# Chunk groups of five across batches, a fifth PSUM bank in the last block, and a new plan for a convolution with two expert layers

## The chip, the cores and the metric

The kernel runs on one NeuronCore of a Trainium2 chip. The metric is device time in microseconds (us) of one execution; lower is better. Times are medians of several runs, and one more execution was recorded by the hardware profiler. Engine names are those of the profile: PE (TensorE matmul), PEld (its weight load), DVE (VectorE), ACT (ScalarE), POOL (GpSimd), SP (SyncE, which issues nearly all DMAs).

## What is computed

The input x is 2 batches of 4096 tokens with 192 channels. Three steps follow each other:

```python
out = np.einsum('hk,bskhg->bshg', softmax(weight), x_unf)      # causal convolution, 7 taps, 8 heads
h = x @ w_in;  g = np.maximum(0.01 * h, h);  x = g @ w_out     # layer 1: 192 -> 2048 -> 192
h = x @ w_in                                                   # layer 2: the same sizes
P = a[0] + a[1] * h + a[2] * h2 + a[3] * h3
Q = 1.0 + np.abs(b[0]) * np.abs(h) + np.abs(b[1]) * h2
out = (P / (Q + 1e-06)) @ w_out
```

Weights come as 64-bit floats, which the kernel converts itself. Every operand of a large matmul is split into a high and a low part, so a product costs several matmuls.

## The kernel before

The 8192 tokens are 16 blocks of 512 (`NB`). For each block i, layer and slice j of 128 of the 2048 hidden columns (16 slices) PE does `gemm1` (5 matmuls of 128x512 into one PSUM tile of the pool `bank`, four tiles), `gemm2_hi` (3 matmuls) and `gemm2_lo` (2 matmuls), both into the accumulators `acc[layer]`. So a block costs 160 matmuls a layer, and the kernel 5120. Block 15's layer 1 accumulates in `acc[0]`.

Between `gemm1` and `gemm2` of layer 2 stand the rational function's steps. For one slice: ACT does `l2_vp` (two instructions), `l2_abs`, `l2_rs`, `l2_R`; DVE does `l2_D`, `l2_p2`, `l2_p3`, `l2_hi`, `l2_r`; POOL does the products `l2_w` and `l2_lo`; `l2_Q` goes to ACT or POOL. `l2_hi` gives the high part for `gemm2_hi` (tile gH), `l2_lo` the low part for `gemm2_lo` (tile gL). The slice's `bank` tile is held from `gemm1` until `l2_r` has read it. In the last block a slice in `GPDEN` takes another way to the denominator: `l2_up` and `l2_t` on ACT and `l2_ut` on POOL stand for `l2_vp`, `l2_D` and `l2_abs`. A slice in `ENDW` may have its `l2_w`, one in `ENDV` its `l2_lo`, on DVE instead of POOL.

`middle` makes block i's layer-2 input from its layer-1 accumulators (`mid_swap`, `x_hi` on ACT; `mid_add`, `x_lo` on DVE); `finish` writes a block out (`fin_swap`, `fin_main`, `fin_add`, `fin_rest`, `fin_store`). Layer 1 of later blocks runs interleaved with layer 2 of earlier ones, so only the end of the kernel has layer 2 alone.

The convolution of blocks 0 and 1 is done directly (`conv`, `trans`). For the others it is done by groups of up to five chunks of 122 tokens: `load_g` (SP), `conv_g` in two halves of four heads (PE, 4 matmuls a half, which the profile shows as 8 records), `evac_g` (ACT), `put_g` (SP, to `y_dram`); `get_y` reads a block back transposed by 32x32 pieces.

The order of all this is not written out. A `Planner` takes every step with a rank (a due time plus an offset from the table `OFF`), its dependencies, its tile pools and a modelled duration, and picks at each moment the step that can start first (`PULL` weighs the rank, `WINDOW` and `LOOK` limit the search). A step that may run on two engines is placed by it too. The `gemm2` of one block depend on each other in the order in which the code lists them. Each engine executes its instructions in the planned order.

`s_warm` and `s_fill` are matmuls without a use but to keep PE busy: 8 of 256 columns and 19 more (`SHAPES`, on a tile filled by `s_seed`) at the start, and single ones at places named in `FEED0` and `FEED`. `s_abs` takes the absolute value of the denominator's coefficients b.

Of the kernel before, what the change touches and what calls it, by code (L numbers as in the profile page):

```python
# [29 lines left out]
WINDOW = 193.974  # L30
LOOK = 58
REST = -0.364
OFF = {'xfin_add': 27.93, 'xfin_main': -41.19, 'l2_rs': -6.51, 'l2_Q': -76.54, 'l2_lo': 20.05, 'cv_clip': 21.93, 'r_lo': -1.28, 'gemm2_lo': -4.32, 'fin_trans': 100.9, 'cv_abs': -25.96, 'gemm2_hi': -3.11, 'l2_R': -14.71, 'cv_low': -5.24, 'fin_evac': -75.01, 'trans': -38.96, 'mid_swap': -4.79, 'x_hi': 22.32, 'conv': -29.75, 'l2_p3': 3.44, 'r_hi': 17.48, 'x_lo': 2.67, 'fin_rest': -19.55, 'l2_abs': 22.74, 'l2_r': 2.84, 'l1_lo': -25.06, 'l2_D': -10.01, 'cv_bits': -8.15, 'l2_hi': -1.95, 'mid_add': -112.83, 'gemm1': -4.61, 'w_lo': -48.12, 'fin_add': -69.89, 'load_g': 63.41, 'conv_g': -23.42, 'evac_g': -35.87, 'put_g': 12.36, 'get_y': -27.55, 'turn_y': 19.29, 'y_hi': -15.46, 'y_lo': -20.59}
TAIL = 5.502
# [139 lines left out]
def conv_leaky_rational_kernel(  # L174
# [302 lines left out]
    def zero_g(eng, g):  # L477
        nc.vector.memset(xt[g % 2][0:K - 1, 0, :], 0.0)

    def conv_g(eng, g, m):  # L480
        k = len(groups[g][1])
# [544 lines left out]
```

## Time and profile before

| | before |
|---|---|
| median of 3 runs | 1244.76 us (1244.41 to 1244.92) |
| profiled execution, its own time | 1244.22 us |
| its span, first to last instruction | 1242.4 us |
| PE busy | 1217.3 us, 98% |
| ACT busy | 1138.5 us, 92% |
| DVE busy | 1112.0 us, 90% |
| POOL busy | 1059.2 us, 85% |
| granted TensorE clock, mean | 0.996 of full speed |

The busy share is an average. PE has hardly any idle time from about 200 to 1160 us; the first 150 us and the last 70 us are where engines wait for each other. A matmul's record (0.39 us) is longer than the distance to the next one, since they overlap; the distance is what counts.

### The profile page before, as it was taken

What the parts mean: (1) busy time and instruction counts of PE and PEld (TensorE: products, weight loads), DVE (VectorE), ACT (ScalarE), POOL (GpSimd) and SP (SyncE); (2) the same over time, 40 slices, a digit from 0 to 9 for tenths busy, and PEclk for the clock granted to TensorE, in tenths of its full rate; (3) what the DMA queues carried; (4) which work ended last, traced back from release to release, by engine and by line L of the source; (5) the groups of instructions that cost most, each with busy time, mean ns of one, the idle gap of its engine ahead of it and who ended that gap; (6) DMA issues with size and microseconds to landing.
All of it is one profiled execution on the core that took longest, in us unless ns stands there. A gap on an engine that the chain in (4) does not pass through costs nothing.

```text
span 1242.4 us, 17891 instructions
## 1 busy us (share of the span) xinstructions
PE 1217.3 (98%) x5437; PEld 997.6 (80%) x5437; DVE 1112.0 (90%) x1671; ACT 1138.5 (92%) x1996; POOL 1059.2 (85%) x1000
## 2 busy tenths in 40 slices
PE   8999999999999999999999999999999999999976
PEld 7787788888888888888888888888888888888744
DVE  7999989898998989898988999898998989889898
ACT  6889999899999999999999999999999999999996
POOL 2787988989889898898888989899898888988886
PEclk9999999999999999999999999999999999999998
DMA  7752002020110201111010111010210002000000
GB/s 210 200 164 71 1 3 52 2 42 1 38 18 1 56 1 44 18 30 33 7 45 12 29 33 29 20 23 5 50 26 1 13 1 41 1 1 14 1 13 13
DMA packets 137414, 42.34 MB, mean 34 GB/s; under 512 B 113571, under 2 KB 134758, under 8 KB 137318
## 3 DMA queue, kind: packets, MB, share of 16 engines
q1 hardware_dynamic: 135702, 41.00, 14.3%
q8 instruction: 42, 0.69, 0.2%
q14 instruction: 54, 0.44, 0.1%
q10 hardware_dynamic: 1616, 0.21, 0.1%
HBM read 27.28 MB, written 11.80 MB: 31 GB/s over the span
## 4 chain that ended last, share of the span: by engine, by line
PE 81%; ACT 7%; DVE 7%; issue 2%; DMA 1%; POOL 1%; SPq 0%; POOLq 0%; DVEq 0%; ACTq 0%
PE bank L253 41%; PE acc L253 39%; ACT work L244 4%; DVE work L250 2%; ACT raw L244 1%; DMA raw<-in_moe_w_in_dram 1%; DVE bank L250 1%; DVE pair L247 1%; ACT bank L244 1%; DVE bank L396 1%; DVE bank L397 1%; DVE pair L250 1%; DVE work L247 0%; DVE raw L250 0%; POOL pair L247 0%
## 5 line engine op out<-in xcount | busy, mean ns | idle before, releaser
L253 PE MATMUL acc<-pair,wo 128*128 128x512 f32 x2560 | 657.4, 391 | 6.2 <-POOL pair L247 2.7
L253 PEld LDWEIGHTS acc<-pair,wo 128*128 128x128 f32 x2560 | 478.5, 188 | 110.6 <-POOL pair L247 6.9
L244 ACT ACTIVATE work<-work 128x512 f32<-128x512 f32 x532 | 331.4, 630 | 17.6 <-DVE work L250 11.0
L247 POOL TENSOR_TENSOR work<-work,pair 128x512 f32<-128x512 f32 x184 | 239.5, 1302 | 43.6 <-DVE pair L250 34.6
L253 PE MATMUL bank<-xh,wiH 128*128 128x512 f32 x512 | 203.5, 397 | 9.2 <-DVE raw L250 4.2
L253 PE MATMUL bank<-xh,wiL 128*128 128x512 f32 x512 | 200.2, 391 | 0.0
L253 PE MATMUL bank<-xl,wiH 128*128 128x512 f32 x512 | 200.0, 391 | 0.0
L253 PE MATMUL bank<-xl,wiR 128*128 128x512 f32 x512 | 200.0, 391 | 0.0
L253 PE MATMUL bank<-xh,wiR 128*128 128x512 f32 x512 | 199.9, 390 | 0.0
L250 DVE SCALAR_TENSOR_TENSOR work<-work,b_sb,bank 128x512 f32<-128x512 f32 x182 | 135.1, 742 | 46.5 <-ACT work L244 45.3
L247 POOL TENSOR_TENSOR pair<-work,work 128x512 fp32r<-128x512 f32 x122 | 158.0, 1297 | 20.4 <-DVE work L250 14.8
L250 DVE SCALAR_TENSOR_TENSOR work<-bank,a_sb,work 128x512 f32<-128x512 f32 x184 | 136.9, 744 | 9.6 <-POOL work L247 7.6
L244 ACT ACTIVATE work<-bank,a_sb 128x512 f32<-128x512 f32 x176 | 135.3, 769 | 6.1 <-PE bank L253 6.0
L250 DVE SCALAR_TENSOR_TENSOR pair<-bank,a_sb,work 128x512 fp32r<-128x512 f32 x168 | 125.2, 745 | 13.1 <-ACT work L244 7.8
L250 DVE SCALAR_TENSOR_TENSOR bank<-work,a_sb,bank 128x512 f32<-128x512 f32 x176 | 132.1, 752 | 4.1
L244 ACT ACTIVATE raw<-raw 128x512 f32<-128x512 f32 x202 | 126.8, 630 | 6.2 <-DVE raw L250 3.6
L253 PEld LDWEIGHTS bank<-xh,wiH 128*128 128x128 f32 x512 | 96.4, 188 | 38.1 <-DVE raw L250 6.6
L247 POOL TENSOR_TENSOR pair<-work,pair 128x512 fp32r<-128x512 f32 x92 | 120.3, 1308 | 7.0 <-PE acc L253 1.8
L244 ACT ACTIVATE work<-bank,b_sb 128x512 f32<-128x512 f32 x182 | 124.0, 681 | 0.0
L247 DVE TENSOR_TENSOR work<-work,bank 128x512 f32<-128x512 f32 x176 | 119.3, 678 | 1.3 <-ACT raw L244 1.3
L253 PEld LDWEIGHTS bank<-xl,wiH 128*128 128x128 f32 x512 | 96.5, 189 | 20.7 <-DVE xl L247 0.3
L253 PEld LDWEIGHTS bank<-xl,wiR 128*128 128x128 f32 x512 | 96.4, 188 | 20.6 <-DVE xl L247 0.3
(104 smaller groups left out, 1954.5 us busy)
## 6 DMA issues: line engine op xcount, KB each, us to landing
work<-y_dram SPq DMA_DIRECT2D x108, 64.0 KB
raw<-in_moe_w_out_dram SPq DMA_DIRECT2D x16, 384.0 KB
xt<-in_x_dram SPq DMA_DIRECT2D x59, 96.0 KB
y_dram<-xc SPq DMA_DIRECT2D x58, 84.0 KB
raw<-in_moe_w_in_dram SPq DMA_DIRECT2D x8, 512.0 KB
out_dram<-work SPq DMA_DIRECT2D x63, 64.0 KB
raw<-in_moe_w_in_dram SPq DMA_DIRECT2D x8, 256.0 KB
work<-work SPq DMA_DIRECT2D x16, 128.0 KB
```

Source lines behind the costliest of these rows:

```text
L244: nc.scalar.activation(out=out_, in_=in_, func=func, **k)
L247: (eng or nc.vector).tensor_tensor(out=out_, in0=in0, in1=in1, op=op)
L250: nc.vector.scalar_tensor_tensor(out=out_, in0=in0, scalar=s, in1=in1, op0=op0, op1=op1)
L253: nc.tensor.matmul(out=out_, lhsT=w, rhs=r, start=start, stop=stop)
L396: nc.vector.tensor_scalar(out=a, in0=a, scalar1=F64_TINY, scalar2=F64_HUGE, op0=ALU.max, op1=ALU.min)
L397: nc.vector.tensor_scalar(out=ai, in0=ai, scalar1=3, scalar2=0x3FFFFFF8, op0=ALU.logical_shift_left, op1=ALU.bitwise_and)
```

## The change

Groups are cut from one list of the 60 chunks of both batches, five at a time: 12 groups of five in place of 13 (eight of five, five of four). `zero_g`, `load_g`, `conv_g`, `evac_g`, `put_g` and `fetch` follow the new form. The start loses `s_seed` and `SHAPES`; `s_warm` issues 13 matmuls of 256 columns in place of 8 and those 19. One accumulator of layer 1, `acc[0][0]`, goes to the pool `bank` once block 15's layer-2 input has been read from it, so the last block has five tiles for h. The rank of `s_abs` goes from -40 to -20. The planner's modelled durations of `conv_g`, of the conversions and of a matmul change slightly. `GPDEN` has six slices instead of four, `ENDW` nine instead of one, `ENDV` six instead of two, and all of the tables and constants are new, so the order of nearly all steps differs.

```diff
-WARM = 8
-SHAPES = ((192, 6, 1), (384, 3, 1), (512, 3, 1), (256, 3, 1), (192, 4, 0))
+WARM = 13
-OFF = {'xfin_add': 27.93, 'xfin_main': -41.19, 'l2_rs': -6.51, 'l2_Q': -76.54, 'l2_lo': 20.05, 'cv_clip': 21.93, ...
+OFF = {'xfin_add': 27.29, 'xfin_main': 2.55, 'l2_rs': -68.95, 'l2_Q': -75.18, 'l2_lo': 7.7, 'cv_clip': 51.44, ...
-GPDEN = (2, 5, 8, 11)
-ENDW = (15,)
+GPDEN = (2, 5, 10, 11, 14, 15)
+ENDW = (2, 3, 4, 5, 6, 8, 9, 12, 13)
-ENDV = (14, 15)
+ENDV = (5, 7, 10, 12, 13, 15)
...
+    pl.pool("own", acc[0][0:1])
...
-    groups = []
+    chunks = []
     for bi in range(B):
-        t0 = max(blocks[DIRECT][3] - bi * S, 0) if bi == 0 else 0
-        count = -(-(S - t0) // CG)
-        starts = [min(t0 + c * CG, S - CG) for c in range(count)]
-        ng = -(-count // NTC)
-        at = 0
-        for g in range(ng):
-            k = min(NTC, -(-(count - at) // (ng - g)))
-            groups.append((bi, starts[at:at + k], t0 + at * CG))
-            at += k
+        t0 = blocks[DIRECT][3] if bi == 0 else 0
+        while t0 < S:
+            s0 = min(t0, S - CG)
+            chunks.append((bi, s0, t0 - s0))
+            t0 = s0 + CG
+    groups = [chunks[c:c + NTC] for c in range(0, len(chunks), NTC)]
...
-    on(DVE(0.4), -83, 0, s_seed, r=["qc"], w=[("xh", 1, 0, 0)])
-    on(PE(0.6 * WARM + 2.2), -74, 0, s_warm, r=["ident", "qc", ("xh", 1, 0, 0)], w=[("acc", 0, 1)])
-    on(ACT(0.2), -40, 0, s_abs, r=["ab"], w=["ab"])
+    on(PE(0.6 * WARM), -74, 0, s_warm, r=["ident", "qc"], w=[("acc", 0, 1)])
+    on(ACT(0.2), -20, 0, s_abs, r=["ab"], w=["ab"])
...
+        if i + 3 == NB:
+            on(POOL(0.01), t1[-1], 9.0, lambda eng: None, w=[("acc", 0, 0), "own"], take=("own", "own"),
+               retire=("own", "bank", lambda t: [t]))
```

Three places show how the planned order moves. The first is ACT where layer 2 begins: `xc` rows are `evac_g` of group 1, the table load stands before the first `l2_rs`. Before:

```order
L244 ACTIVATE work_110<-bank_99,a_sb 128x512
L244 ACTIVATE work_113<-bank_99,b_sb 128x512
L244 ACT_TABLE_LOAD
L244 ACTIVATE work_114<-work_105 128x512
L244 ACTIVATE xc<-bank_101 122x5x96
L244 ACTIVATE work_114<-work_114 128x512
L244 ACTIVATE work_107<-acc_98 64x512 x2
L244 ACTIVATE xc<-bank_100 122x5x96
```

And now, in two pieces, the earlier one first:

```order
L244 ACTIVATE work_112<-bank_99 128x512
L244 ACTIVATE work_110<-raw_126 128x384
L244 ACTIVATE pair_116<-work_112 128x512
L244 ACTIVATE xc<-bank_101 122x5x96
L244 ACTIVATE wo_75<-work_104 128x2x192
L244 ACTIVATE xc<-bank_99 122x5x96
```

```order
L244 ACTIVATE work_114<-bank_101,a_sb 128x512
L244 ACTIVATE work_106<-bank_101,b_sb 128x512
L244 ACTIVATE bank_102<-bank_102 128x512
L244 ACTIVATE pair_116<-bank_102 128x512
L244 ACTIVATE work_106<-work_106 128x512
L244 ACT_TABLE_LOAD
L244 ACTIVATE work_104<-work_106 128x512
```

Both evacuations have moved from behind the table load to well ahead of it.

The second place is PE at the end of layer 1: `acc00`, `acc01` are layer 1's accumulators, `xh100` is block 14's layer-2 input, `xh101` block 15's, `acc10`, `acc11` are layer 2's accumulators. Before, from the last `gemm2` of layer 1 on:

```order
L253 MATMUL acc01_96<-pair8_124,wo0_74 128x512
L253 MATMUL acc00_95<-pair8_124,wo0_74 128x512
L253 MATMUL acc10_97<-pair5_121,wo1_75 128x512 x2
L253 MATMUL acc11_98<-pair5_121,wo1_75 128x512
L253 MATMUL acc11_98<-pair3_119,wo1_75 128x512
L253 MATMUL acc10_97<-pair3_119,wo1_75 128x512
L253 MATMUL acc10_97<-pair2_118,wo1_75 128x512 x2
L253 MATMUL acc11_98<-pair2_118,wo1_75 128x512
L253 MATMUL acc11_98<-pair4_120,wo1_75 128x512
L253 MATMUL acc10_97<-pair4_120,wo1_75 128x512
L253 MATMUL acc10_97<-pair0_116,wo1_75 128x512 x2
L253 MATMUL acc11_98<-pair0_116,wo1_75 128x512
```

Behind these comes the last block's first `gemm1`. Now there are ten more matmuls at this place, the last `gemm1` of block 14 among them:

```order
L253 MATMUL acc10_97<-pair0_116,wo1_75 128x512 x2
L253 MATMUL acc11_98<-pair0_116,wo1_75 128x512
L253 MATMUL acc11_98<-pair2_118,wo1_75 128x512
L253 MATMUL acc10_97<-pair2_118,wo1_75 128x512
L253 MATMUL bank2_101<-xh100_83,wiH1_69 128x512
L253 MATMUL bank2_101<-xh100_83,wiL1_71 128x512
L253 MATMUL bank2_101<-xl100_91,wiH1_69 128x512
L253 MATMUL bank2_101<-xh110_85,wiR1_73 128x512
L253 MATMUL bank2_101<-xl110_93,wiR1_73 128x512
L253 MATMUL acc10_97<-pair6_122,wo1_75 128x512 x2
L253 MATMUL acc11_98<-pair6_122,wo1_75 128x512
```

Block 14's last `gemm1` has moved behind layer 1's end, and layer 1's end ten matmuls ahead; the last block's first `gemm1` keeps its place (4,953 large matmuls stand ahead of it in both).

The third place is the kernel's end. On DVE, before, from slice 15's `l2_hi` (`pair1`) to its `l2_lo` (`pair8`):

```order
L250 SCALAR_TENSOR_TENSOR pair1_117<-bank0_99,a_sb_65,work11_114 128x512
L250 SCALAR_TENSOR_TENSOR raw0_126<-bank2_101,a_sb_65,raw0_126 128x512
L247 TENSOR_TENSOR raw2_128<-raw2_128,pair1_117 128x512
L250 SCALAR_TENSOR_TENSOR raw2_128<-bank0_99,a_sb_65,raw2_128 128x512
L247 TENSOR_TENSOR pair8_124<-raw2_128,work11_114 128x512
```

Now, from slice 15's `l2_hi` (`pair7`) to the `l2_lo` of slices 12 (`pair2`) and 15 (`pair3`):

```order
L250 SCALAR_TENSOR_TENSOR pair7_123<-bank3_102,a_sb_65,work5_108 128x512
L250 SCALAR_TENSOR_TENSOR work12_115<-bank0_99,a_sb_65,work12_115 128x512
L247 TENSOR_TENSOR work2_105<-work2_105,pair6_122 128x512
L250 SCALAR_TENSOR_TENSOR work2_105<-bank1_100,a_sb_65,work2_105 128x512
L250 SCALAR_TENSOR_TENSOR raw0_126<-bank3_102,a_sb_65,raw0_126 128x512
L247 TENSOR_TENSOR pair2_118<-raw2_128,work8_111 128x512
L247 TENSOR_TENSOR pair3_119<-raw0_126,work5_108 128x512
```

On PE, before, the `gemm2_lo` of slices 13, 14 and 15 (`pair9`, `pair6`, `pair8`) end the list:

```order
L253 MATMUL acc01_96<-qc_67,ident_61 128x256
L253 MATMUL acc11_98<-pair9_125,wo1_75 128x512
L253 MATMUL acc10_97<-pair9_125,wo1_75 128x512
L253 MATMUL acc11_98<-pair6_122,wo1_75 128x512
L253 MATMUL acc10_97<-pair6_122,wo1_75 128x512
L253 MATMUL acc11_98<-pair8_124,wo1_75 128x512
L253 MATMUL acc10_97<-pair8_124,wo1_75 128x512
```

Now the `gemm2_lo` of slice 12 (`pair2`), behind it the `gemm2_hi` of 13, 14 and 15 (`pair6`, `pair8`, `pair7`), and then the `gemm2_lo` of 13 (`pair5`), which those of 14 and 15 follow:

```order
L253 MATMUL acc01_96<-qc_67,ident_61 128x256
L253 MATMUL acc11_98<-pair2_118,wo1_75 128x512
L253 MATMUL acc10_97<-pair2_118,wo1_75 128x512
L253 MATMUL acc10_97<-pair6_122,wo1_75 128x512 x2
L253 MATMUL acc11_98<-pair6_122,wo1_75 128x512
L253 MATMUL acc10_97<-pair8_124,wo1_75 128x512 x2
L253 MATMUL acc11_98<-pair8_124,wo1_75 128x512
L253 MATMUL acc10_97<-pair7_123,wo1_75 128x512 x2
L253 MATMUL acc11_98<-pair7_123,wo1_75 128x512
L253 MATMUL acc11_98<-pair5_121,wo1_75 128x512
L253 MATMUL acc10_97<-pair5_121,wo1_75 128x512
```

DVE's last product but one is now slice 12's, and 17 matmuls of PE stand in order behind it, where two stood behind DVE's last product.

## Rows read from the trace of the kernel before

**Rows 1.** The page, part 1: busy us (share of span) xinstructions.

```profile
PE 1217.3 (98%) x5437; PEld 997.6 (80%) x5437; DVE 1112.0 (90%) x1671; ACT 1138.5 (92%) x1996; POOL 1059.2 (85%) x1000
```

**Rows 2.** Windows (length; PE, PEld, DVE, ACT, POOL busy; clock, DMA): middle, two of the tail.

```profile
200.00:1160.00 960.00, 959.83 (x4310) 794.91 (x4309) 860.76 (x1274) 895.76 (x1561) 847.40 (x786) 1.00 0.10 21
1176.76:1232.67 55.91, 44.24 (x159) 30.04 (x157) 52.43 (x81) 53.47 (x90) 48.75 (x43) 0.94 0.04 8
1178.21:1236.08 57.87, 45.52 (x163) 31.04 (x163) 54.35 (x83) 52.03 (x88) 50.33 (x44) 0.94 0.04 8
```

**Rows 3.** Timeline of PE (start, us, what), halves of five-chunk and four-chunk groups.

```profile
488.59 1.04 PE L253 MATMUL bank<-xt,band 128*122 128x120 f32 x8
489.39 1.41 PE L253 MATMUL acc<-pair,wo 128*128 128x512 f32 x5
...
1025.77 0.99 PE L253 MATMUL bank<-xt,band 128*122 128x96 f32 x8
1026.54 0.94 PE L253 MATMUL acc<-pair,wo 128*128 128x512 f32 x3
```

**Rows 4.** Timeline where layer 2 begins: ACT, then PE.

```profile
105.23 1.28 ACT L244 ACT_TABLE_LOAD   x1
...
107.06 0.55 ACT L244 ACTIVATE xc<-bank 122x480 f32<-122x480 f32 x1
...
109.38 0.57 ACT L244 ACTIVATE xc<-bank 122x480 f32<-122x480 f32 x1
...
107.67 0.50 PE L253 MATMUL bank<-xh,wiH 128*128 128x512 f32 x1 [0.28 <-ACT xc L244]
...
110.00 0.50 PE L253 MATMUL bank<-xh,wiH 128*128 128x512 f32 x1 [0.91 <-ACT xc L244]
```

**Rows 5.** Timeline of PE at the kernel's start.

```profile
2.50 5.70 PE L253 MATMUL acc<-qc,ident 128*128 128x256 f32 x16 [2.50 <-POOL ident masks.py:199]
7.84 3.01 PE L253 MATMUL acc<-xh 128*128 128x192 f32 x19
12.22 2.09 PE L253 MATMUL bank<-xt,band 109*103 109x120 f32 x16 [1.36 <-DMA b_sb<-in_moe_b_dram]
```

**Rows 6.** Timeline where the last block's layer 2 begins: PE, ACT, DVE.

```profile
1170.72 4.47 PE L253 MATMUL acc<-pair,wo 128*128 128x512 f32 x19
1175.03 0.39 PE L253 MATMUL bank<-xh,wiH 128*128 128x512 f32 x1
...
1176.76 0.78 ACT L244 ACTIVATE work<-bank,a_sb 128x512 f32<-128x512 f32 x1 [0.33 <-PE bank L253]
...
1178.21 0.74 DVE L250 SCALAR_TENSOR_TENSOR work<-work,b_sb,bank 128x512 f32<-128x512 f32 x1
```

**Rows 7.** DVE's groups by form (busy us, mean ns); then DVE, POOL in the timeline.

```profile
L247 DVE TENSOR_TENSOR xl<-work,xh 128x512 fp32r<-128x512 f32 x14 | 13.8, 984 | 0.0
L247 DVE TENSOR_TENSOR xl<-acc,xh 128x512 fp32r<-128x512 f32 x16 | 11.0, 686 | 0.0
...
148.82 1.81 DVE L247 TENSOR_TENSOR xl<-raw,xh 128x512 fp32r<-128x512 f32 x1
...
1233.82 1.72 POOL L247 TENSOR_TENSOR pair<-raw,work 128x512 fp32r<-128x512 f32 x1
```

**Rows 8.** Timeline of PE in the tail, slices 4 to 5.

```profile
1191.32 0.79 PE L253 MATMUL bank<-xh,wiH 128*128 128x512 f32 x1 [1.60 <-DVE raw L250]
1191.91 0.63 PE L253 MATMUL bank<-xh,wiL 128*128 128x512 f32 x1
1192.34 0.63 PE L253 MATMUL bank<-xl,wiH 128*128 128x512 f32 x1
```

**Rows 9.** Timeline at the kernel's end: DVE's last product, PE, ACT.

```profile
1235.29 0.79 DVE L247 TENSOR_TENSOR pair<-raw,work 128x512 fp32r<-128x512 f32 x1
...
1235.59 1.29 PE L253 MATMUL acc<-pair,wo 128*128 128x512 f32 x4 [0.74 <-POOL pair L247]
...
1236.68 0.59 ACT L244 ACTIVATE work<-acc 64x512 f32<-64x512 f32 x1 [4.00 <-PE acc L253]
```

More of the change, by code (lines that the diff above doesn't have):

```diff
@@ L19 @@
 SIZES = [512] * 16
-LEAD = 66.057
-GAP = 6.373
-PREP = 56.276
+LEAD = 70.459
+GAP = 10.982
+PREP = 39.883
 AHEAD = 40.0
-WARM = 8
-SHAPES = ((192, 6, 1), (384, 3, 1), (512, 3, 1), (256, 3, 1), (192, 4, 0))
+WARM = 13
 WIDE = 256
 FILL = {'conv': 1, 'trans': 1}
-STEP = 4.016
+STEP = 4.139
 PULL = 0.005
[L30 to L34, printed above, removed]
+WINDOW = 222.069
+LOOK = 43
+REST = -1.826
+OFF = {'xfin_add': 27.29, 'xfin_main': 2.55, 'l2_rs': -68.95, 'l2_Q': -75.18, 'l2_lo': 7.7, 'cv_clip': 51.44, 'r_lo': -28.86, 'gemm2_lo': -5.41, 'fin_trans': 128.42, 'cv_abs': -27.82, 'gemm2_hi': -1.77, 'l2_R': -20.86, 'cv_low': -13.55, 'fin_evac': -104.18, 'trans': -60.4, 'mid_swap': 22.99, 'x_hi': 19.14, 'conv': -12.52, 'l2_p3': -4.13, 'r_hi': 41.3, 'x_lo': 26.01, 'fin_rest': -3.03, 'l2_abs': 21.56, 'l2_r': 8.13, 'l1_lo': -8.77, 'l2_D': -14.35, 'cv_bits': 28.75, 'l2_hi': -15.24, 'mid_add': -56.69, 'gemm1': -4.99, 'w_lo': -14.13, 'fin_add': -122.45, 'load_g': 21.72, 'conv_g': -32.45, 'evac_g': -27.81, 'put_g': 90.79, 'get_y': -18.62, 'turn_y': 52.41, 'y_hi': -10.45, 'y_lo': -2.7}
+TAIL = 4.702
 FIN = 3.219
-CV1, CV2, CV3 = -20.785, 58.237, 26.634
+CV1, CV2, CV3 = -25.775, 147.141, 33.724
 EVERY, INPLACE = 2, (1,)
@@ L468, in load_g @@
     def load_g(eng, g):
-        bi, starts, _ = groups[g]
         t = xt[g % 2]
-        for c, s0 in enumerate(starts):
+        for c, (bi, s0, _) in enumerate(groups[g]):
             if s0 == 0:
@@ L477, in zero_g @@
     def zero_g(eng, g):
[L478 removed]
+        for c, (bi, s0, _) in enumerate(groups[g]):
+            if s0 == 0:
+                nc.vector.memset(xt[g % 2][0:K - 1, c, :], 0.0)
     def conv_g(eng, g, m):
[L481 removed]
+        k = len(groups[g])
         pv = buf[("gps", g, m)][0:CG, 0:k * HC].rearrange("p (t c) -> p t c", t=k)
@@ L492, in put_g @@
     def put_g(eng, g):
-        bi, starts, t0 = groups[g]
-        for c, s0 in enumerate(starts):
-            rows = s0 + CG - (t0 + c * CG)
+        for c, (bi, s0, done) in enumerate(groups[g]):
+            rows = CG - done
             r0 = B * S - bi * S - s0 - CG
@@ L818, in group @@
     def group(g):
-        bi, starts, _ = groups[g]
-        k, p = len(starts), g % 2
-        first = next(i for i in range(NB) if blocks[i][3] + blocks[i][2] > bi * S + groups[g][2])
+        k, p = len(groups[g]), g % 2
+        first = next(i for i in range(NB) if blocks[i][3] + blocks[i][2] > spans[g][0])
         base = t1[first * NJ] - AHEAD
         xk = ("xt", p)
-        if starts[0] == 0:
+        if any(s0 == 0 for _, s0, _ in groups[g]):
             on(DVE(0.25), base - 50, 2.0, zero_g, g, w=[xk])
@@ L836, in fetch @@
         base = t1[i * NJ] - AHEAD
-        yk = [("y", g) for g, (bi, starts, t0) in enumerate(groups)
-              if bi * S + t0 < tok0 + n and bi * S + starts[-1] + CG > tok0]
+        yk = [("y", g) for g, (a, z) in enumerate(spans) if a < tok0 + n and z > tok0]
         for m in range(2):
@@ L851, in prep @@
         if i >= DIRECT:
-            while made[0] < len(groups) and groups[made[0]][0] * S + groups[made[0]][2] < blocks[i][3] + blocks[i][2]:
+            while made[0] < len(groups) and spans[made[0]][0] < blocks[i][3] + blocks[i][2]:
                 group(made[0])
```

22 lines of the change are left out of this document (8 added, 14 removed).

## The prediction, made before the changed kernel ran

> **What bounds the kernel now.** I read the page's busy times first: PE is busy 98% of the span, the others 85 to 92% [rows 1]. That is an average, so I then cut the span into windows. From 200 to 1160 us PE is busy 959.8 of 960 us [rows 2]: there only fewer matmuls help, and nothing that ACT, DVE or POOL do differently is seen as long as it stays within their slack (ACT 64, DVE 99, POOL 113 us of 960). In the tail it is the other way round: from 1176.76 to 1232.67 ACT is busy 53.5 of 55.9 us, DVE 52.4, POOL 48.8 and PE 44.2 [rows 2]. The tail is a chain of elementwise work with three engines nearly full, and PE waits. Third, I read the places where PE waits in the first 150 us [rows 4, 5]. So the change can act in three ways: fewer matmuls, other waits at the start, another tail.
>
> One matmul of the large kind costs 0.227 us of PE: 19 of them stand from 1170.72 to the next one's start at 1175.03 [rows 6].
>
> **The group that goes.** A half of a five-chunk group takes 0.80 us from its start to the next matmul's (488.59 to 489.39), a half of a four-chunk group 0.77 (1025.77 to 1026.54) [rows 3]. The time hardly depends on the number of chunks, so 12 groups of five cost what 12 of the 13 did, and two halves go: 1.6 us, with the slower first matmul behind a half up to 1.8. PE has no slack there, so all of it counts: **-1.7 us**. The two evacuations that go with it (0.55 and 0.57 us on ACT [rows 4]) and the new edge between the batches lie in ACT's and SP's slack: nothing. The number of chunks, and so of DMAs, is the same.
>
> **The start.** The coefficients' later rank changes nothing that I can find: `s_abs` stands at the same place in ACT's order and its DMA at the same place in SP's. The warm-up gets shorter. 16 records of the first kind took 5.70 us and the 19 others lasted to 10.85; then PE stood 1.36 us until the convolution's `band` had landed at 12.22 [rows 5]. The ten records that are added cost 0.36 us each at most (5.70/16), so the new warm-up ends by 11.4 at the latest and perhaps a us earlier, and PE stands 0.8 to 2 us. The landing sets the 12.22, so this costs nothing unless the clock falls before it, which is a bound of +1.5 (the 2.09 us of these convolutions taking 1.5 us more). The first certain gain is at layer 2's beginning: ACT loads a table for 1.28 us, evacuates group 1 behind it (107.06 and 109.38), and PE waits 0.28 and 0.91 us for these two tiles [rows 4]. Now both evacuations come well ahead of the table load, so **-1.2 us**. PE's other waits up to 170 us are small ones; with nearly every step moved, new ones come as old ones go. I take -0.3 for them, and as bounds twice what the table load cost, -2.5 and +2.5. Start in all: **-1.5**, from -4 to +2.5.
>
> **The tail, from the last block's first `gemm1` on.** As many matmuls stand ahead of it in both plans, so its start (1175.03) moves only by what was said above. From there I add up DVE's path, since DVE gets the most work.
>
> Step 1, when DVE begins on the block. Before, ACT starts the block's first slice at 1176.76 and DVE at 1178.21, 3.2 us behind the `gemm1` [rows 6]. Now block 14's last `gemm1` comes only 8 matmuls (1.8 us) before it, so ACT still has that slice's five instructions to do, two of which wait for DVE in between. At 0.6 us an instruction (53.47 us for 90 [rows 2]) that puts DVE's begin about 4.4 us behind: **+1.2**; bounds 0 (ACT gets through in time) and +1.5.
>
> Step 2, the number of DVE's instructions. From its first `l2_D` of the block to its last `l2_lo` it had 82, and now has 85: two `l2_D` less, five products more. At 54.35/83 = 0.655 us each [rows 2]: **+2.0**.
>
> Step 3, what a product costs on DVE. `x_lo` with one input in PSUM takes 0.686 us in the mean; the same instruction with both inputs in SBUF takes 0.984, and one next to POOL's work took 1.81 [rows 7]. A POOL product that met one on DVE took 1.72 us. The products that now go to DVE read two SBUF tiles, and POOL is busy 48.8 of 55.9 us. Five more at 0.30 each: **+1.4**; bounds 0 and 5 x 1.1 = 5.6. (The Trainium skill, "SBUF — State Buffer", section "Who interferes with whom", says that a DVE instruction with two SBUF inputs and a GpSimd instruction that reads SBUF exclude each other for a whole instruction. The trace agrees: 1.81 us in place of 0.69 on DVE, and 1.72 on POOL. By that rule alone this step would lie between its two bounds, and it speaks against moving products to DVE beside a full POOL.)
>
> Step 4, DVE's idle time. It had 57.87 - 54.35 = 3.5 us of it [rows 2], most of it in wait for a full ACT or for a `gemm1` that waited for a PSUM tile. ACT loses 6 of 90 instructions (nine `l2_Q` become three), 3.6 us, and a fifth tile stands in for the wait of 1.60 us at 1191.32, behind which the `gemm1` ran at half distance, 0.43 us [rows 8]. I take three quarters of the idle time off: **-2.6**; bounds -3.5 and +1.
>
> Step 5, the drain. Before, PE's last matmul ends by 1236.68, 0.6 us after DVE's last product (1235.29 + 0.79) [rows 9]. Now DVE's last but one is slice 12's `l2_lo`, and the order of the accumulation holds 17 matmuls behind it: 17 x 0.227 = 3.9 us, counted from 0.65 before DVE's end, so 3.3 us against 0.6: **+2.7**. This is the one term that the order alone makes certain. If they run at half clock, 17 x 0.43 = 7.3: +3.4 more.
>
> Tail: 1.2 + 2.0 + 1.4 - 2.6 + 2.7 = +4.7. What follows PE's end (the block's output) is the same.
>
> **Sum.** -1.7 - 1.5 + 4.7 = +1.5 us. Against the profiled execution, 1244.22 us, that is 1245.7; against the median of 1244.76 it is **1246.2 us**, which I give. About 0.2% (2.5 us) is what a measurement of this kernel can tell from no change, so the forecast is no change, on the slow side.
>
> **Rivals.**
>
> (a) The drain runs cold (slower). PE has only fills to do while DVE works off its last six products and sums, so its clock may fall to 1.2 GHz as it did behind the wait at 1191.32 [rows 8] (granted clock of the tail 0.94 [rows 2]), and the 17 matmuls then take 7.3 us: 1246.2 + 3.4 = 1249.6 us. It decides if PE stands idle ahead of slice 12's `gemm2_lo` as it did there. For it: DVE's last stretch is 3.9 us long. Against it: a drain of four matmuls at the end before ran at full distance (1.29 us [rows 9]). Step 3 near its upper bound would give as much alone.
>
> (b) The fifth tile and the lighter ACT let the tail run without gaps (faster). DVE's idle time goes whole (-3.5), DVE begins as early as before, the products slip between POOL's at no price, and the start gives 3 us: -1.7 - 3 + 2.0 - 3.5 + 2.7 = -3.5, so 1241.2 us. For it: ACT was the fullest engine there and loses most. Against it: the drain is in the order and cannot slip away, and DVE goes from 54 to over 55 us of work in 58.
>
> (c) The plan does not do what the words say. For the coefficients this is so, and is in the sum at nothing. The fifth tile is used: `acc00` takes `gemm1`s of the last block in PE's order.
>
> **How the numbers follow.** Forecast, within 0.2%: 0.45. Slower by more, mostly (a) or step 3 above its middle: 0.37. Faster by more, (b): 0.18. Time 1246.2. The range takes in most of (a) and (b), with a little left out on each side: 1241.6 to 1250.0; the forecast's own range is 1242.3 to 1247.2.
>
> **What would show it.** Group: 24 `conv_g` halves of some 0.78 us, and PE's busy time in the middle as full as before. Start: no wait of PE for `xc` at layer 2's beginning, and the last block's first `gemm1` at about 1172 (right if between 1171 and 1174). Tail: DVE's first instruction of the last block 4 to 5 us behind that; seven products on DVE in the tail with a mean of 0.8 to 1.0 us; DVE's idle time there under 2 us; 17 matmuls behind slice 12's `l2_lo`, 3.9 us at full clock. I am wrong if the first `gemm1` of the last block comes before 1169 or after 1176 (then the start decided), or if PE's end follows DVE's by less than 2 us.

## The result, and the profile after

| | before | after |
|---|---|---|
| median, 4 runs each (the three of before and one more) | 1244.6 us | 1260.1 us |
| ratio, 95% interval | | 1.0121 (1.0106 to 1.0136) |
| span of the profiled execution | 1242.4 us | 1258.5 us |

The change made the kernel 15.5 us slower; the forecast was 1246.2, the range ended at 1250.0. First the page's busy times after, which answer to [rows 1], then windows (length; PE, PEld, DVE, ACT, POOL busy; clock, DMA) that answer to [rows 2]: the middle, the tail from DVE's first instruction of the last block to its last, and the drain.

```profile
PE 1220.9 (97%) x5412; PEld 997.8 (79%) x5412; DVE 1111.4 (88%) x1678; ACT 1131.9 (90%) x1976; POOL 1064.4 (85%) x1010
```

```profile
200.00:1160.00 960.00, 957.42 (x4271) 786.40 (x4270) 854.99 (x1280) 888.99 (x1544) 841.58 (x781) 1.00 0.10 20
1184.99:1247.26 62.27, 41.90 (x146) 29.61 (x145) 58.54 (x85) 49.19 (x82) 51.69 (x47) 0.87 0.04 7
1246.71:1252.81 6.10, 6.10 (x17) 4.67 (x17) 0.55 (x1) 0.00 (x0) 0.00 (x0) 0.62 0.00 0
```

PE's busy time in the middle fell by 2.4 us only, and its records overlap, so a wait that is shorter than a record's overhang isn't seen there at all. I therefore counted loss by starts: the distance between two `gemm1`, less 0.2267 us for each large matmul between them and 0.775, an estimate after [rows 3], for each half of a group. From block 4's first `gemm1` of layer 1 to block 14's first of layer 2 that is, before, 1106.71 - 245.67 - 3713 x 0.22667 - 20 x 0.775 = 3.9 us; after, 1109.59 - 243.50 - 3715 x 0.22667 - 18 x 0.775 = 10.1 us. I call it the **middle's loss**. The four `gemm1` that it is counted between, first before, then after:

```profile
245.67 0.39 PE L253 MATMUL bank<-xh,wiH 128*128 128x512 f32 x1
1106.71 0.39 PE L253 MATMUL bank<-xh,wiH 128*128 128x512 f32 x1
```

```profile
243.50 0.39 PE L253 MATMUL bank<-xh,wiH 128*128 128x512 f32 x1
1109.59 0.39 PE L253 MATMUL bank<-xh,wiH 128*128 128x512 f32 x1
```

I put the loss down to the matmul ahead of which it arises, leaving out those right behind a half of a group. After the change eleven `gemm1` start 0.04 to 0.90 us late, 3.7 us in sum, and the second matmul of each some 0.1 us more, 1.2 in sum; before, it was one `gemm1`, by 0.33 and 0.11. All of them start 0.05 to 0.06 us behind the end of the last read of the PSUM tile that they take over. So 4.5 of the 6.1 us that PE loses more in the middle are waits for a free tile. The whole difference, in the order of time:

| stretch | after against before, us |
|---|---|
| first `gemm1` (17.83, now 19.14) | +1.31 |
| from there to block 4's first `gemm1`, loss 10.12 before, 8.91 after | -1.21 |
| two halves of a group fewer, at 0.775 each | -1.55 |
| middle's loss | +6.14 |
| from there to the last block's first `gemm1`, loss 0.31 before, 2.43 after | +2.12 |
| tail, from that `gemm1` to `fin_swap`, 61.65 before, 70.98 after | +9.33 |
| what follows | -0.05 |
| span | +16.1 |

The start: PE's timeline (start, us, what, in brackets the idle time ahead and what ended it), which answers to [rows 5], and a window of four us.

```profile
2.40 7.37 PE L253 MATMUL acc<-qc,ident 128*128 128x256 f32 x26 [2.40 <-POOL ident masks.py:199]
12.05 3.29 PE L253 MATMUL bank<-xt,band 109*103 109x120 f32 x16 [2.28 <-DMA b_sb<-in_moe_b_dram]
...
19.14 0.53 PE L253 MATMUL bank<-xh,wiH 128*128 128x512 f32 x1
```

```profile
12.00:16.00 4.00, 3.95 (x20) 3.85 (x21) 1.03 (x3) 1.40 (x4) 0.00 (x0) 0.57 0.98 245
```

The shorter warm-up left PE idle for 2.28 us where it was 1.36, and the granted clock was 0.57 behind it. In the middle, one of the two largest losses (0.87 us by starts; POOL, DVE, PE):

```profile
261.07 1.29 POOL L247 TENSOR_TENSOR raw<-raw,pair 128x512 f32<-128x512 f32 x1
...
261.43 1.48 DVE L247 TENSOR_TENSOR xl<-raw,xh 128x512 fp32r<-128x512 f32 x1
...
264.28 0.50 PE L253 MATMUL bank<-xh,wiH 128*128 128x512 f32 x1 [0.71 <-DVE raw L250]
```

An `x_lo` with two SBUF inputs takes 1.48 us beside POOL's `l2_w`, `l2_r` comes late, and PE waits for the PSUM tile that it frees. The end of layer 1, where PE waits for a product of POOL (block 14's `l2_lo` of slice 13):

```profile
1180.57 1.43 PE L253 MATMUL acc<-pair,wo 128*128 128x512 f32 x5 [1.30 <-POOL pair L247]
```

The tail's begin (against [rows 6]), then its longest wait and its end (against [rows 8, 9]):

```profile
1181.83 0.39 PE L253 MATMUL bank<-xh,wiH 128*128 128x512 f32 x1
...
1183.62 0.76 ACT L244 ACTIVATE work<-bank,a_sb 128x512 f32<-128x512 f32 x1
...
1184.99 0.75 DVE L250 SCALAR_TENSOR_TENSOR work<-work,b_sb,bank 128x512 f32<-128x512 f32 x1 [0.46 <-ACT work L244]
```

```profile
1226.34 0.80 PE L253 MATMUL bank<-xh,wiH 128*128 128x512 f32 x1 [5.84 <-DVE work L250]
1226.94 0.63 PE L253 MATMUL bank<-xh,wiL 128*128 128x512 f32 x1
...
1245.12 2.13 DVE L247 TENSOR_TENSOR pair<-raw,work 128x512 fp32r<-128x512 f32 x2
...
1246.71 6.30 PE L253 MATMUL acc<-pair,wo 128*128 128x512 f32 x17 [4.53 <-DVE pair L247]
...
1252.81 0.59 ACT L244 ACTIVATE work<-acc 64x512 f32<-64x512 f32 x1 [12.41 <-PE acc L253]
```

DVE begins 3.16 us behind the `gemm1` (3.18 before). It works for 58.54 us (54.36), idles for 3.72 (3.51), and `fin_swap` comes 5.56 us behind its last product (0.60): 3.16 + 58.54 + 3.72 + 5.56 = 70.98. The 17 matmuls stand behind a wait of 4.53 us and run mostly at 0.43 us, half clock.

### The profile page after: what moved, and what is told of

It is laid out like the page before. It is cut to its first block, busy times and chain, and to the rows that moved or that the text cites. A ratio compares the mean times of both kernels' runs of the same rounds, so it can differ in the third digit from the quotient of the medians.

```text
span 1258.5 us, 17814 instructions
## 1 busy us (share of the span) xinstructions
PE 1220.9 (97%) x5412; PEld 997.8 (79%) x5412; DVE 1111.4 (88%) x1678; ACT 1131.9 (90%) x1976; POOL 1064.4 (85%) x1010
## 4 chain that ended last, share of the span: by engine, by line
PE 80%; ACT 8%; DVE 5%; issue 2%; POOL 1%; ACTq 0%; DVEq 0%; POOLq 0%
PE bank L253 41%; PE acc L253 39%; ACT work L244 5%; ACT raw L244 2%; DVE pair L250 1%; DVE raw L250 1%; DVE work L250 1%; DVE work L247 1%; DVE bank L250 1%; ACT pair L244 0%; DVE pair L247 0%; POOL pair L247 0%; POOL raw L247 0%; ACT bank L244 0%; DVE xl L247 0%
## 5 line engine op out<-in xcount | busy, mean ns | idle before, releaser
L253 PE MATMUL acc<-pair,wo 128*128 128x512 f32 x2560 | 643.7, 392 | 8.6 <-DVE pair L247 5.8
L244 ACT ACTIVATE work<-work 128x512 f32<-128x512 f32 x481 | 299.3, 628 | 20.6 <-DVE work L250 13.4
L247 POOL TENSOR_TENSOR work<-work,pair 128x512 f32<-128x512 f32 x157 | 207.8, 1324 | 38.2 <-DVE pair L250 31.7
L253 PE MATMUL bank<-xh,wiH 128*128 128x512 f32 x509 | 203.7, 400 | 16.0 <-DVE work L250 11.4
L250 DVE SCALAR_TENSOR_TENSOR work<-work,b_sb,bank 128x512 f32<-128x512 f32 x157 | 116.4, 741 | 46.2 <-ACT work L244 45.5
L247 POOL TENSOR_TENSOR pair<-work,work 128x512 fp32r<-128x512 f32 x110 | 143.4, 1307 | 15.7 <-DVE work L250 10.3
L250 DVE SCALAR_TENSOR_TENSOR pair<-bank,a_sb,work 128x512 fp32r<-128x512 f32 x184 | 136.8, 744 | 17.5 <-ACT work L244 11.0
L244 ACT ACTIVATE work<-bank,a_sb 128x512 f32<-128x512 f32 x181 | 139.5, 771 | 11.9 <-PE bank L253 11.1
L247 POOL TENSOR_TENSOR raw<-raw,pair 128x512 f32<-128x512 f32 x95 | 123.7, 1302 | 22.9 <-DVE pair L250 18.0
L244 ACT ACTIVATE raw<-raw 128x512 f32<-128x512 f32 (+1 forms) x205 | 127.6, 627 | 10.8 <-DVE raw L250 9.0
L250 DVE SCALAR_TENSOR_TENSOR work<-bank,a_sb,work 128x512 f32<-128x512 f32 x160 | 119.0, 744 | 4.7 <-POOL work L247 3.8
L253 PEld LDWEIGHTS bank<-xh,wiR 128*128 128x128 f32 x509 | 96.1, 189 | 20.5
```

The costliest lines, as they stand in the source:

```text
L244: nc.scalar.activation(out=out_, in_=in_, func=func, **k)
L247: (eng or nc.vector).tensor_tensor(out=out_, in0=in0, in1=in1, op=op)
L250: nc.vector.scalar_tensor_tensor(out=out_, in0=in0, scalar=s, in1=in1, op0=op0, op1=op1)
L253: nc.tensor.matmul(out=out_, lhsT=w, rhs=r, start=start, stop=stop)
```

## Experiments

**The tail: the lists.** My theory was that `GPDEN`, `ENDW` and `ENDV` make it long; the rival, that the offsets do. The lists were taken out of the changed kernel, and put alone into the kernel before with groups and tile; the order ahead of the last block stays.

```diff
-GPDEN = (2, 5, 10, 11, 14, 15)
-ENDW = (2, 3, 4, 5, 6, 8, 9, 12, 13)
-ENDV = (5, 7, 10, 12, 13, 15)
+GPDEN = (2, 5, 8, 11)
+ENDW = (15,)
+ENDV = (14, 15)
```

> The changed kernel with the lists GPDEN, ENDW and ENDV as before; the order is the changed kernel's up to the last block's fourth slice. Theory (the lists make the tail long): its 71.0 us from the last block's first gemm1 to the last read of its sums fall to 59 to 63, and the time from 1260.1 to 1248 to 1252. Rival (the changed offsets do): 66 us or more, time 1255 or more.

Measured: 1251.8 us, 8.3 less than with the changed lists; the tail fell from 70.98 to 61.97. The reverse edit:

> The kernel before with groups of five and the fifth tile (1243.05 us), and in addition the changed lists GPDEN, ENDW and ENDV; the order is that kernel's up to the last block's seventh slice. Theory (the changed lists are what makes the tail long: more products on DVE beside POOL, slice 12's late product with matmuls behind it): from the last block's first gemm1 to the last read of its sums it takes 58.9 us without and 63 to 70 with them; the time is 1247 to 1254. Rival (the lists are harmless with the old offsets; the changed offsets and the changed TAIL make the tail long): 1242.5 to 1245.

Measured: 1251.1 us, 8.1 more; the tail rose from 58.93 to 67.01. DVE's stretch of the tail in the first of these kernels (DVE 58.54 us with the changed lists, above), then in the second, without the changed lists and with them:

```profile
1184.65:1242.75 58.10, 46.35 (x159) 33.70 (x159) 53.93 (x81) 52.10 (x87) 51.61 (x46) 0.85 0.04 7
```

```profile
1182.47:1237.63 55.16, 43.13 (x163) 28.79 (x163) 53.93 (x83) 50.79 (x87) 50.53 (x45) 1.00 0.04 8
1180.21:1241.45 61.24, 47.81 (x154) 33.09 (x155) 58.56 (x85) 49.48 (x84) 51.83 (x45) 0.83 0.04 7
```

Either way the lists put 4.6 us on DVE (58.54 - 53.93; 58.56 against 53.93 without) and, with the offsets as changed, take 2.9 off ACT. DVE's idle time goes another way: without the changed lists it is 1.23 us with the old offsets and 4.17 with the changed ones, with them 2.68 and 3.72. So the tail is settled: nearly all of its loss is the lists', in either kernel.

**The drain.** One step of PE's order was moved:

```diff
+    ahead(("gemm2_lo", 1, 15, 12), ("gemm2_lo", 1, 15, 13))
```

> The changed kernel with one step moved in PE's order: slice 12's gemm2_lo stands behind slice 15's gemm2_hi, ahead of slice 13's gemm2_lo, so 8 matmuls stand behind DVE's last products and not 17. Theory (the drain behind slice 12's product is PE's own): PE ends 1.9 us (full clock) to 3.5 us (half clock) behind the start of that gemm2_lo at 1246.7, where it now ends 6.1 us behind; the time falls by 2.6 to 4.2 us, to 1256 to 1257.5. Rival (the drain's length doesn't matter, because DVE's last product at 1247.3 and what follows it set the end): less than 0.5 us.

Measured: 1256.3 us, 3.8 less. Nine matmuls now run ahead of DVE's last products, and eight behind, at full clock (granted 1.00):

```profile
1240.28 2.43 PE L253 MATMUL acc<-pair,wo 128*128 128x512 f32 x9
1245.22 2.11 PE L253 MATMUL acc<-pair,wo 128*128 128x512 f32 x8 [2.51 <-DVE pair L247]
```

**The wait of 5.84 us.** It looks like the tail's largest loss.

> The changed kernel with four steps of the last block moved forward: on POOL l2_w of slice 8 ahead of l2_ut of slice 10 and l2_w of slice 9 ahead of that of slice 10, on DVE l2_r of slice 8 ahead of l2_hi of slice 9 and l2_r of slice 9 ahead of that of slice 10. So the PSUM tiles of slices 8 and 9 come free some 8 us earlier, and PE's wait of 6.00 us ahead of slice 13's gemm1 should fall under 2 us. Theory (DVE's work sets the tail, PE's wait runs beside it): only DVE's idle time, 3.6 us in the tail, can shrink, and the time falls by 1 to 2.5 us. Rival (the wait for the tile sets the tail): the time falls by 4 to 6 us.

Measured: 1259.7 us, no change, and the wait was 7.0 us. My edit missed: slice 13's `gemm1` had been given slice 10's tile, not slice 8's. With the tiles reassigned, and the drain's edit:

> The changed kernel with three edits of the last block: slice 12's gemm2_lo behind slice 15's gemm2_hi on PE; l2_w and l2_r of slices 8 and 9 earlier on POOL and DVE; and slices 13, 14 and 15 take the PSUM tiles of slices 8, 9 and 10 in place of those of 10, 11 and 8, which alone lets PE use what comes free earlier. The first edit alone took 3.8 us. Theory (DVE's work sets the tail): PE's wait of 6 us ahead of slice 13's gemm1 goes, DVE's idle time falls from 3.7 us by 1 to 2, and the time is 1254 to 1255.5. Rival (the wait for the tile sets the tail): 1250 to 1252.5. Or neither, DVE's idle time only moves: 1256 to 1257.

Measured: 1255.5 us, 0.8 less than the drain's edit alone, which is within the spread of those runs (1254.9 to 1258.4); the tail in the profiled executions is 1.1 us shorter (65.67 against 66.81). The wait is 1.92 us,

```profile
1222.64 0.50 PE L253 MATMUL bank<-xh,wiH 128*128 128x512 f32 x1 [1.92 <-DVE work L250]
```

and DVE's idle time fell from 3.69 (with the drain's edit alone) to 2.53. Four us of PE's wait were worth one: DVE's work sets the tail.

**The products on DVE.**

```diff
-        tt(d, d, f(b("gH", 1, i, j)), ALU.mult, nc.gpsimd if eng == "POOL" else nc.vector)
+        if eng == "DVE":
+            return tt(d, d, acc[0][1], ALU.mult)
```

> The changed kernel with the second operand of seven instructions replaced: in the last block, l2_w of slices 4, 6, 12, 13 and l2_lo of slices 10, 12, 15, which DVE does, read a PSUM tile (layer 1's second accumulator) in place of the second SBUF tile. This leaves these seven products out; the number of instructions and the order are the same. Theory (two SBUF inputs beside POOL's work cost DVE 0.4 us each): the seven take 0.69 us in the mean and not 1.08, DVE's last product ends 2 to 3 us earlier, and the time falls by as much. Rival (POOL's products set DVE's end there, so the time on DVE is hidden): under 1 us.

Measured: 1258.6 us, 1.5 less, where the theory had 2 to 3; the tail is 1.75 us shorter (69.23). DVE's timeline:

```profile
1238.20 0.69 DVE L247 TENSOR_TENSOR pair<-work,acc 128x512 fp32r<-128x512 f32 x1 [1.16 <-PE acc L253]
1239.68 0.69 DVE L247 TENSOR_TENSOR raw<-raw,acc 128x512 f32<-128x512 f32 x1
```

All seven take 0.68 to 0.69 us; in the changed kernel their sum is 7.59 us, here 4.78. The 2.8 us are the second SBUF input's; 1.2 of them went into a wait for PE that the borrowed PSUM tile brought. (The Trainium skill, "SBUF — State Buffer", section "Who interferes with whom": a DVE instruction with at most one SBUF input, outside the 2-port modes, does not contend with GpSimd. The run agrees: POOL's products at 1241.96 and 1243.18, on either side of the one at 1242.42, took 1.27 us each; in the changed kernel the two-input product at 1242.38 took 1.38, and the POOL product that met it 1.72.)

**The fifth tile and the groups, without the new numbers.** The tile alone:

```diff
+    pl.pool("own", acc[0][0:1])
...
+        if i + 3 == NB:
+            on(POOL(0.01), t1[-1], 9.0, lambda eng: None, w=[("acc", 0, 0), "own"], take=("own", "own"),
+               retire=("own", "bank", lambda t: [t]))
```

> The kernel before with the fifth PSUM tile alone: every engine's order is that of before up to the last block's fourth slice. Theory (the tile takes waits for a gemm1 out of the tail): DVE's idle time from its first l2_D of the last block to its last product falls from 3.5 us to 1.2, as it did beside the groups of five, DVE begins as before, the drain stays at 0.6 us, and the time falls by 2.0 to 2.7 us, to 1241.6 to 1242.4. Rival (DVE's work of 54.4 us sets the tail and the idle time comes back elsewhere): 1243.7 to 1244.6.

Measured: 1242.5 us, ratio 0.9988 (0.9979 to 0.9997): faster than both kernels. DVE's idle time fell from 3.51 to 1.52 us and the tail from 61.65 to 59.36. DVE's stretch of it:

```profile
1179.80:1235.41 55.61, 44.48 (x163) 30.04 (x163) 54.09 (x83) 50.72 (x87) 50.62 (x45) 0.97 0.04 8
```

With the groups of five too:

> The kernel before with two parts of the change alone: the chunk groups of five and the fifth PSUM tile for the last block; tables, lists of slices, warm-up, durations and the rank of s_abs are those of before. Theory (the new tables and lists cost the time, not the groups or the tile): the groups give 1.6 us, the tile up to 1.5, PE's loss between 200 and 1160 us is 3 us as before, and the time is 1241 to 1244. Rival (the groups that reach across the batches or the tile that is taken from layer 1 bring the waits): 1248 or more, with PE's loss in the middle or the tail's length near the changed kernel's.

Measured: 1243.1 us, ratio 0.9990 (0.9980 to 1.0000). The middle's loss is 6.5 us, against 3.8 with the tile alone: the groups save 1.6 us of halves and bring 2.7 of waits. My theory holds for the time, not for the middle.

**The middle.** Six ideas in turn, each on the loss of 10.1 us. The rank of `l2_rs`, which puts it ahead of layer 1's `l1_hi` on ACT:

> The changed kernel with one number of its table of ranks as before: l2_rs -6.51 in place of -68.95. The order of the whole middle and of the tail changes with it. Theory (with l2_rs first on ACT, layer 1's l1_hi comes later, its PSUM tiles are held longer, and PE waits for tiles): the mean time from a layer-1 gemm1 to its l1_hi falls from 4.3 us to about 3.3, and what PE loses between 200 and 1160 us, 8.4 us now and 3.0 before the change, falls to 4 to 6; the time falls by 2 to 5 us unless the tail gets another length. Rival (PE's waits in the middle come from the products on DVE that read two SBUF tiles beside POOL's work): these stay as many, and the loss stays at 7 to 9 us.

Measured: `l1_hi` came at 3.45 us as forecast, the loss stayed (10.5 us). The time was 1257.7 us, 2.4 less, which the tail explains: its order changed too, and it got 3.3 us shorter. The theory fell.

The two-input products (`order[q] = (n, "POOL")` for them):

> The changed kernel with 27 products that read two SBUF tiles moved from DVE to POOL, at the same places of the order: the 13 y_lo and the 14 x_lo of the second half of layer 2's input, blocks 2 to 15. Theory (where such a product meets one on POOL it takes 1.4 to 1.8 us and not 0.7, DVE comes late with l2_r, and PE waits for the PSUM tile): PE's waits at 264 us (0.87) and 883 us (0.90) go, the loss between 200 and 1160 us falls from 8.4 to 6 or less, and the time falls by 2 to 3 us. Rival (the order keeps the tiles too long, whatever DVE's products take): the loss stays at 7.5 to 9 us, other waits take the place of these, and the time stays within 1 us.

Measured: 1262.1 us, loss 11.1. The waits at 264 and 883 us went, and others came (waits from 200 to 1160 us: total, times, longest):

```profile
PE bank L253 <- DVE work L250: 1.1, 3, 0.4
PE acc L253 <- POOL pair L601: 0.9, 1, 0.9
PE bank L253 <- DVE pair L247: 0.6, 2, 0.4
```

The rival was right on the loss and the waits. The time is 2.0 us up and not within 1; in the profiled execution the first `gemm1` came 2.2 us later (21.29), behind a start at half clock. The same edit in the kernel with groups and tile:

> The kernel before with groups of five and the fifth tile (1243.05 us), and in addition the y_lo and the x_lo of the second half of layer 2's input (blocks 2 to 15) on POOL where they stood on DVE. Theory (PE's waits of 1.29 us at 569 and 0.94 us at 1037 stand behind an x_lo of 1.63 and of 1.53 us): PE's loss between 200 and 1160 us falls from 5.5 to 3.5 or less, and the time is 1240.5 to 1242. Rival (POOL, with 88% of the middle busy, gets 18 us more and comes late with l2_w and l2_lo): no gain or 1 to 3 us slower.

Measured: 1243.4 us, loss 6.4 (6.5 without): a wait of 1.3 us for a POOL product took the place of the two. The blocked products decide where PE waits, not how long in sum.

The offsets:

> The changed kernel with the table of offsets OFF as before; its constants, lists and code are the changed ones. Theory (the new offsets keep each slice's PSUM tile longer, so that PE finds no free tile): the mean time from a layer-1 gemm1 to its l1_lo, 5.3 us now and 4.0 before, is about 4, that from a layer-2 gemm1 to its l2_r, 10.8 now and 10.5 before, at most 10.5, and what PE loses from block 4's first gemm1 of layer 1 to block 14's of layer 2, 10.1 us now and 3.9 before, falls to 4 to 6.5; the time falls by 3 to 6 us if the tail keeps its length. Rival (the constants for the two layers' pace, the window and the groups cause it): the loss stays at 9 to 11 us.

Measured: 1265.9 us, loss 10.6, though odd `l1_lo` came 3.4 us behind `gemm1` (4.9 in the changed kernel) and `l2_r` 10.3. The longest waits are others (245 to 1106 us):

```profile
PE acc L253 <- DVE xl L247: 1.0, 3, 0.4
PE bank L253 <- DVE pair L247: 0.3, 1, 0.3
```

The planner's durations:

> The changed kernel with the planner's durations of a matmul, of conv_g and of the conversions as before; the order of the whole changes with them. Theory (with a matmul counted longer than it is, the plan leaves PE waiting: 0.0004 us for each of some 3,300 matmuls from block 4 to block 14, and more where steps were placed by it): PE's loss from block 4's first gemm1 of layer 1 to block 14's of layer 2 falls from 10.1 us to 5 to 7, the time to 1254 to 1257. Rival (the loss belongs to the numbers of the tables and any new plan with them has it): 9 to 12 us or more, time 1258 to 1264.

Measured: 1266.7 us, loss 12.0. The tables and constants alone, in the kernel before:

> The kernel before with the changed table of offsets and the changed constants of pace, window and conversion (OFF, LEAD, GAP, PREP, STEP, WINDOW, LOOK, REST, TAIL, CV1 to CV3) alone: groups, tiles, lists of slices and warm-up are those of before. Theory (these numbers alone make PE's waits in the middle): what PE loses from block 4's first gemm1 of layer 1 to block 14's of layer 2 rises from 3.9 us to 8 to 10, and the time rises by 5 to 9 us with what the tail adds. Rival (the groups or the planner's changed durations make them): 3 to 5.5 us of loss, and a time within 3 us of before.

Measured: 1270.2 us, 25.7 more than before; loss 23.1, one wait of 4.0 us for `fin_main` among it. Where the kernels with the old offsets and with the old durations lose most against the changed one is the stretch ahead of block 4: 17.0 and 13.9 us, against 8.9. So the new numbers are worse in the old code than in the new, the old numbers in the new code (offsets, durations) are worse than either whole set: numbers and code belong together, and no single one of those tried carries the 6 us.

Last, the time that a slice keeps its tile. A layer-2 slice keeps it until `l2_r`, an odd slice of layer 1 until `l1_lo`. In the traces `l2_r` comes 10.5 us behind `gemm1` before and 10.8 after, an odd `l1_lo` 3.4 and 4.9. The median time from the end of a tile's last read to the next `gemm1` on it is 1.92 us before and 1.13 after, and it is under 0.3 us in 2.4% of 372 and 13.1% of 373 cases.

> The kernel before with the fifth tile (1242.5 us), and from block 3 on each odd layer-1 slice's l1_hi two instructions later on its engine, its l1_lo behind it; nothing else moves. The order of PE is the same. Theory (how long a slice keeps its PSUM tile decides what PE loses in the middle): the mean time from an odd layer-1 gemm1 to its l1_lo goes from 3.4 to 4.7 us, as in the changed kernel (4.9), the loss from block 4's first gemm1 of layer 1 to block 14's of layer 2 from 3.8 to 6 to 9 us, and the time rises by 2 to 5 us. Rival (the tiles have time to spare; the changed kernel's waits come from something else in its order): 3.5 to 5 us of loss, the time within 1 us.

> The kernel before with the fifth tile (1242.5 us), and in blocks 1 to 13 each layer-2 slice's l2_r, which lets go of the PSUM tile, two instructions later on DVE; nothing else moves. Theory (how long a slice keeps its PSUM tile decides what PE loses in the middle): the mean time from a layer-2 gemm1 to its l2_r goes from 10.5 to 11.5 us or so (10.8 in the changed kernel), the loss from block 4's first gemm1 of layer 1 to block 14's of layer 2 from 3.8 to 8 us or more, and the time rises by 4 us or more. Rival (the tiles have time to spare): 3.5 to 5.5 us of loss, the time within 2 us.

In a few of the moved slices (2 of 104, 17 of 208) the moved step now stands behind the matmul that takes its tile over, and reads the next values there. Measured: 1316.5 and 1347.9 us, losses 69.8 and 98.2. The waits of the first, from 245 to 1106 us, PE's and DVE's:

```profile
PE bank L254 <- DVE pair L248: 35.2, 41, 2.3
```

```profile
DVE pair L248 <- ACT pair L245: 88.0, 83, 2.1
```

In both, PE waits for tiles, and steeply. But the edits did more than I meant: DVE itself waited 88 us for the moved `l1_hi`, so everything behind came late too. And the mean hold alone doesn't set the loss: in the first, an odd `l1_lo` came 5.0 us behind `gemm1`, near the changed kernel's 4.9, with seven times its loss. They don't show that the longer hold is the cause in the changed kernel, and the run with the old offsets, short holds and a loss of 10.6, speaks against its being the only one. That PE waits for tiles is shown by the starts above; **what in the plan makes them come late stays open** between its numbers.

**The start.** Six more useless matmuls in the changed kernel:

> The changed kernel with 19 useless matmuls at the start in place of 13, in an order that is otherwise the same. Theory (PE stands 2.28 us ahead of the first convolution and its clock falls, granted clock 0.57 from 12 to 16 us): PE works to about 11.8, the granted clock from 12 to 16 us is 1.00, the convolution's first 16 records take 2.1 us and not 3.3, the first gemm1 starts at 17.9 and not 19.14, and the whole takes 1.3 us less, about 1258.8. Rival (the start is made up for by later waits, for weights that land no sooner): the first gemm1 comes earlier, but at the 40th us the gain is gone, and the time stays within 0.4 us.

Measured: 1257.4 to 1260.2 us, no gain: the first `gemm1` came at 19.24. The clock held, but the warm-up overran the landing:

```profile
2.40 11.39 PE L253 MATMUL acc<-qc,ident 128*128 128x256 f32 x38 [2.40 <-POOL ident masks.py:199]
13.62 1.81 PE L253 MATMUL bank<-xt,band 109*103 109x120 f32 x16
```

Neither theory: the warm-up's own matmuls cost what the clock gave. Five short ones in the fastest kernel:

```diff
-SHAPES = ((192, 6, 1), (384, 3, 1), (512, 3, 1), (256, 3, 1), (192, 4, 0))
+SHAPES = ((192, 6, 1), (384, 3, 1), (512, 3, 1), (256, 3, 1), (192, 9, 0))
```

> The kernel before with the fifth tile (1242.52 us), and five more useless matmuls of 192 columns at the start; the order is otherwise the same. Theory (where PE stood 1.65 us or longer ahead of the first convolution its clock fell, where it stood 1.46 us or less it held): PE stands 0.5 to 0.7 us, the clock holds in every run, the runs above 1244 us go, and the median falls by 0 to 0.6 us. Rival (the spread of these runs comes from later transfers): the same spread, and a median within 0.3 us.

Measured: 1242.7 us, ratio 0.9988 (0.9979 to 0.9997), runs from 1241.7 to 1244.1 (1241.7 to 1245.7 without). In the profiled execution the landing came late (12.89), PE still stood 1.50 us, and the clock held. The median is the same; whether the spread is smaller for this reason is open.

## Why the prediction was wrong

**The step that failed** is the sentence that from 200 to 1160 us nothing that ACT, DVE or POOL do differently is seen as long as it stays within their slack. Their slack in the middle hardly changed (ACT 71 us, DVE 105), and PE lost 6.1 us more. 4.5 of them are waits for a PSUM tile to come free, and no term stood for that: the sum has one for new waits up to 170 us alone. Those 6.1 us, and 2.1 more at layer 1's end, where PE now waits 1.30 us for a POOL product, are 8.3 of the 14.6 us by which the forecast (+1.5) missed the span's growth (+16.1): the last block's first `gemm1` came at 1181.83, not at 1172. Which numbers of the plan free the tiles late stays open. (The Trainium skill, "Perfetto Trace Analysis", section "Optimization Strategy", takes the same gap repeating on the engine that should be full as a sign that tiles may be short. Here no gap repeats: the eleven waits ahead of a `gemm1` last 0.04 to 0.90 us and come at uneven distances.)

**The group**, -1.7: right in that two halves went (192 records of five chunks, 24 halves), though by [rows 3] 16 halves at 0.80 and 10 at 0.77 less 24 at 0.80 are 1.3 us, not 1.6. And the order around them is not free; with the old numbers it brought 2.7 us of waits.

**The start**, -1.5: the waits of 0.28 and 0.91 us for `xc` went, as forecast, and the loss up to block 4 fell by 1.2. The clock's bound, which I left at nothing, was paid in this execution: +1.3. (Ten records at 0.36 us behind 8.20 are 11.8, not the 11.4 that I gave as the warm-up's latest end; it ended at 9.77.)

**The tail**, +4.7, was 9.3. Step 1, +1.2: DVE began as early as before, 0. Steps 2 and 3, +3.4: 4.2, since the seven products took 1.08 us in the mean (7.59/7), not 0.95 (and five at 0.30 are 1.5, not 1.4). Step 4, -2.6: +0.2. The term is near for the tile alone (-2.0, and -2.3 beside the groups), but ACT's lighter load didn't add to it, and the changed order took it back: with the changed offsets DVE idles for 4.17 us even without the changed lists. Step 5, +2.7: 5.0. **Rival (a)** happened: PE stood idle for 4.53 us ahead of the 17 matmuls, clock 0.62. Its condition was in front of me: the products that PE waits for were all DVE's last, and nothing but fills stood between.

Rival (b)'s mechanism, the fifth tile, is real: by itself it makes the kernel 2 us faster. I took the whole change as one; the tile, the groups and the lists, put in one after the other, are -2.0, +0.5 (within the noise) and +8.1. The shorter warm-up and the rank of `s_abs` were not put in alone.

The `Planner` had said some of it. Run without the chip, it starts the last step at 1224.5 us before and 1232.9 after (+8.4, up to 2.0 of it because it counts a matmul 0.0004 us longer; measured +15.5), 1.5 us earlier with the tile alone (measured -2.0), 4.0 later with the lists on top of tile and groups (+8.1), and 14.3 later with the new numbers in the old code (+25.7). It has the signs, and roughly half of the sizes. It was not right for the old durations, which change its own model: 0.7 us earlier than after, measured 6.7 later.

## What to carry to other kernels

An engine's average slack says nothing of the chain that frees a scarce buffer: look at the time between a tile's last reader and its next writer, and the share of cases in which it is nearly nothing. A table of tuned numbers belongs to the code that it was found with; put the code's parts in first, each alone. At an end that an elementwise engine sets, count the matmuls behind its last product, and let accumulation steps that are late in any case go last.
